# A two-part block (windowed attention, then token and channel mixing) on one core: the first attention tile in two halves of heads, conversions at other places in tiles 0, 7 and 8, and five clamps on GpSimd

## The chip, the cores and the metric

The kernel runs on one core of one Trainium2 chip. The metric is the device time of one execution in microseconds (us). The kernel before took 800.99 us, the median of three runs (800.95 to 801.45). The engines are called as in the profile: PE (matrix products), ACT (activations and copies), DVE (vector operations), POOL (GpSimd), SP (issues DMA transfers; ACT can issue them too).

## The reference

Eight sequences of 576 tokens with 8 heads of 64. First attention with a window of 64 tokens; then a mixing step over tokens (`w_tok1`, 576 to 256, and `w_tok2`, back), and one over channels (`w_ch1`, 512 to 1536, and `w_ch2`, back). All data are float32.

```python
scores = scale * np.matmul(q, k.transpose(0, 1, 3, 2))
mask = (rel >= 0) & (rel < window)                 # rel = query position - key position
scores = np.where(mask, scores, -1e9)
scores = scores - np.max(scores, axis=-1, keepdims=True)
attn = np.exp(scores)
attn = attn / (np.sum(attn, axis=-1, keepdims=True) + 1e-09)
x = np.matmul(attn, v)                             # heads side by side: (8, 576, 512)
h = np.maximum(xt @ w_tok1, 0.0) @ w_tok2          # xt is x with tokens and channels exchanged
u = x + h.transpose(0, 2, 1)
out = u + np.maximum(u @ w_ch1, 0.0) @ w_ch2
```

The four weights arrive as float64, as pairs of 32-bit words, and the kernel makes float32 numbers of them on the chip.

## The kernel before

**Attention in 36 tiles.** A tile is two blocks of 64 queries with all 8 heads; nine tiles hold a pair of sequences. One pass of the loop over `i` works on several tiles at once, and the order of the instructions on each engine is the order in which the loop writes them: every engine runs its own list in order and waits where its operand isn't there. For tile `i`:

- `qk` (L282) makes the scores on PE into two PSUM tiles `s` of four heads each: u=0 the even heads, u=1 the odd ones.
- `softmax` (L297) masks, negates and takes the row minimum of each head on DVE: one instruction for a head and a short one that reads out the minimum `nm`.
- `softmax_exp` (L305) makes the exponentials `e` on ACT, one instruction per head, with the row sums.
- `pt_transpose` transposes `e` on PE (L312, into `pp`) and copies it to SBUF on ACT (L314, `pt`).
- `av` multiplies by v on PE (L324, `xp`, in the PSUM slot "av"); `recip` (L333 on POOL in tiles 0 to 6, L336 on DVE) and `norm` (L341 on DVE) give the attention output `x`.
- `split_x` makes `xhi` on ACT (L109) and `xlo` on POOL (L112). `tok1` (L372, PE) adds the tile to the two PSUM banks `h` of its sequence with three products per bank. When a sequence is complete, `finish_h` (L383) takes the positive part of both banks to `hhi` on ACT, and `finish_h_low` (L392) the remainder `hlo` on DVE, which frees the banks. From tile 9 on `tok2` (L413, L420, PE; L425, ACT) makes the mixed tokens `u` from it, through one PSUM slot "up".

**Weight pieces.** Between the tiles the weights are converted in 28 pieces of 320 or 384 columns; `JOBS` says in which pass. Pieces 0 to 4 are converted in passes 0 to 4, pieces 5 and 6 in passes 7 and 8. A piece takes six DVE instructions: L204 (strip the sign), L206 (the clamp: a maximum and a minimum with constants), L207 (shift), L216, L218, L219; then POOL adds two parts to `w` (L221). In the next pass `job_finish` splits `w` into `t1hi` or `t2hi` on ACT (L109) and the remainder `t1lo` on POOL or `t2lo` on DVE (L112). On ACT this split stands ahead of that pass's exponentials. The first three DVE steps of a piece (L204, L206, L207) are `job_convert_a`, the last three (L216, L218, L219, with the sum `w` on POOL) `job_convert_b`; in passes below `N_START` = 7 both stand behind `norm`, in passes from 7 on both ahead of it.

**Stages behind it.** From about 250 us on come the channel products in two ways (three plain chunks, then pairs of chunks by a scheme with seven products in place of eight); the change doesn't touch them.

**The start.** SP loads q of tile 0, the k blocks of tile 0, q of tile 1, the k blocks of tile 1 and so on, while PE runs five products of zeros (L481).

Of the kernel before, what the change touches and what calls it, by code (L numbers as in the profile page):

```python
# [22 lines left out]
P = 128  # L23
# [24 lines left out]
N_START = 7  # L48
# [42 lines left out]
def mixer_kernel(ctx: ExitStack, tc: tile.TileContext, qh, kh, vh, wt1, wt2, wc1, wc2, out):  # L91
# [39 lines left out]
    with ExitStack() as actx:  # L131
# [64 lines left out]
        def to_f32_a(raw, n, tag, late=False):  # L196
# [9 lines left out]
            nc.vector.tensor_scalar(out=cf, in0=cf, scalar1=F64_LOW, scalar2=F64_HIGH, op0=ALU.max, op1=ALU.min)  # L206
            nc.vector.tensor_scalar(out=c, in0=c, scalar1=3, scalar2=0x3FFFFFFF,  # L207
                                    op0=ALU.logical_shift_left, op1=ALU.bitwise_and)
            return c, low, high, n, tag, late
# [31 lines left out]
        def job_convert_a():  # L241
            if to_convert:
                n, raw = to_convert.pop(0)
                to_convert_b.append((n, to_f32_a(raw, jobs[n][4], n, n >= N_FIRST)))
# [24 lines left out]
        def qk(i):  # L269

            qt = loaded[i][0]
            s = []
            for u in range(2):

                s.append(ps.tile([P, 4, P], F32, name=f"s{i}_{u}", tag="h" if i == 1 else "s", bufs=2))
                s_ps[i, u] = s[u]
            for j in range(4):
                for u in range(2):
                    r = slice(u * BLK, (u + 1) * BLK)
                    for half, (b, n) in enumerate(tile_blocks(i)):  # L280
                        so = s[u][half * BLK:(half + 1) * BLK, j].rearrange("p (n c) -> p n c", n=2)
# [3 lines left out]
        def softmax(i, u):  # L285
            if u == 0:
# [4 lines left out]
            e = pa.tile([P, 4, P], F32, name=f"e{i}_{u}", tag="e", bufs=4)  # L291
            e_sb[i, u] = e

            s = s_ps.pop((i, u))
            for h in range(4):
                g = 2 * h + u
                nc.vector.tensor_tensor_reduce(out=e[:, h], in0=s[:, h], in1=mk, scale=-scale, scalar=MAX_F32,  # L297
                                               op0=ALU.add, op1=ALU.min, accum_out=nm[:, g:g + 1])

        def softmax_exp(i, u):  # L300
            e = e_sb[i, u]
            nm, sm = st[i]
            for h in range(4):
                g = 2 * h + u
# [158 lines left out]
        load_q(0)  # L463
# [19 lines left out]
        for i in range(-1, NT + 1):  # L483
# [59 lines left out]
            for n in tok1_plan.get(i + 1, ()):  # L543
                if n not in xhl:
                    split_x(n)
# [548 lines left out]
```

## Time and profile before

| What | Value |
|---|---|
| median of three runs | 800.99 us |
| profiled execution | 801.79 us, of which the span of its instructions is 799.8 us |
| PE busy | 787.4 us, 98% of the span |
| DVE, ACT, POOL busy | 71%, 49%, 33% |
| granted PE clock | 1.00 in every window up to 800 us |
| PE busy in 5 to 45 us | 36.78 of 40.00 us |
| PE busy in 45 to 75 us | 27.24 of 30.00 us |
| PE busy in 75 to 250 us | 174.15 of 175.00 us |

A row of the timeline gives start and duration in us, engine, source line, operation, output<-inputs by the program's names, the shapes, and in brackets how long the engine had stood idle and what ended that. A row of the list of waits gives the sum of the idle time, how often, and the longest. An engine that waits behind another one's hold on the SBUF counts as busy.

### The profile page before, as it was taken

To read this page: it belongs to the slowest core of one execution; us is meant where nothing else is said; L and a number is where in the kernel's file an instruction comes from. 1 tells how busy PE (TensorE), PEld (TensorE's weight loads), DVE (VectorE), ACT (ScalarE), POOL (GpSimd) and SP (SyncE) were. 2 spreads that over 40 slices of the span, in tenths; PEclk is the share of its full clock that TensorE was granted. 3 is DMA by queue.
4 is the path that set the end of the run, shared out by engine and by line. 5 is a ranking of instruction groups with operands and counts; after the bars stand their busy time and mean duration, and the time that the engine had idled before them with its cause. 6 is when DMAs were issued, how large, how long until landed. Compare 5 with 4: busy or idle time off the path is not lost.

```text
span 799.8 us, 15811 instructions
## 1 busy us (share of the span) xinstructions
PE 787.4 (98%) x5749; PEld 654.8 (82%) x5749; DVE 570.2 (71%) x1533; ACT 388.3 (49%) x1124; POOL 262.5 (33%) x237
## 2 busy tenths in 40 slices
PE   8999999999999999999999999999999999999997
PEld 6667888888889888888888888888888888888886
DVE  5978789589582795777788474757766667656576
ACT  6999889889874441323334141326332244324040
POOL 3634545445330000000000050549732638723140
PEclk9999999999999999999999999999999999999999
DMA  9856779668635537877655775765985756955543
GB/s 352 282 179 229 235 251 304 223 217 308 218 113 170 197 103 216 257 225 235 207 164 193 275 289 184 258 236 203 294 320 201 288 187 207 349 209 191 201 159 105
DMA packets 86828, 180.59 MB, mean 226 GB/s; under 512 B 8800, under 2 KB 51808, under 8 KB 84832
## 3 DMA queue, kind: packets, MB, share of 16 engines
q1 hardware_dynamic: 84640, 177.76, 64.4%
q10 hardware_dynamic: 2112, 1.84, 0.7%
q8 instruction: 45, 0.74, 0.4%
q14 instruction: 31, 0.25, 0.1%
HBM read 137.69 MB, written 41.88 MB: 225 GB/s over the span
## 4 chain that ended last, share of the span: by engine, by line
PE 93%; ACT 3%; DVE 3%; POOL 1%; issue 1%; DVEq 0%; ACTq 0%
PE op L969 22%; PE gp L913 21%; PE op L643 12%; PE gp L635 12%; PE up L420 6%; PE h L372 6%; PE xp L324 4%; PE s L282 3%; PE pp L312 3%; PE up L413 3%; ACT e L305 2%; DVE e L297 1%; PE idle L481 1%; DVE x L341 1%; POOL xlo L112 0%
## 5 line engine op out<-in xcount | busy, mean ns | idle before, releaser
L913 PE MATMUL gp<-m,w1hi 128*128 128x512 f32 x504 | 155.1, 389 | 0.0
L112 POOL TENSOR_TENSOR m7lo<-t3g,m7hi 128x512 fp32r<-128x512 f32 x18 | 23.4, 1300 | 359.4 <-ACT m7hi L109 359.4
L305 ACT ACTIVATE e<-e,nm 128x128 f32<-128x128 f32 x288 | 112.3, 398 | 5.7 <-DVE nm L297 5.7
L913 PEld LDWEIGHTS gp<-m,w1hi 128*128 128x128 f32 x504 | 94.6, 188 | 19.6
L913 PE MATMUL gp<-m,w1lo 128*128 128x512 f32 x252 | 98.0, 389 | 0.0
L958 DVE TENSOR_TENSOR uf<-op,uf 128x512 f32<-128x512 f32 (+1 forms) x91 | 61.9, 684 | 39.5 <-PE op L969 31.7
L297 DVE CUSTOM_DVE_ANT_0 e<-s,mask 128x128 f32<-128x128 f32 x288 | 63.5, 286 | 12.5 <-PE s L282 12.4
L112 POOL TENSOR_TENSOR xlo<-x,xhi 128x512 fp32r<-128x512 f32 x32 | 41.2, 1289 | 46.3 <-ACT xhi L109 46.0
L305 ACT ACTIVATION_READ_ACCUMULATOR e<-e,nm 128x1 f32 x288 | 56.3, 196 | 0.0
L635 PE MATMUL gp<-ulo,w1hi 128*128 128x512 f32 x144 | 56.0, 389 | 0.0
L635 PE MATMUL gp<-uhi,w1hi 128*128 128x512 f32 x144 | 56.0, 389 | 0.0
L635 PE MATMUL gp<-uhi,w1lo 128*128 128x512 f32 x144 | 56.0, 389 | 0.0
L913 PEld LDWEIGHTS gp<-m,w1lo 128*128 128x128 f32 x252 | 47.3, 188 | 9.9
L916 ACT COPY x<-gp 128x512 f32<-128x512 f32 x18 | 10.6, 588 | 80.8 <-PE gp L913 80.8
L643 PE MATMUL op<-glo,w2hi 128*128 128x512 f32 x128 | 49.8, 389 | 0.0
L643 PE MATMUL op<-ghi,w2hi 128*128 128x512 f32 x128 | 49.8, 389 | 0.0
L643 PE MATMUL op<-ghi,w2lo 128*128 128x512 f32 x128 | 49.8, 389 | 0.0
L221 POOL TENSOR_TENSOR w<-r,c 128x384 f32<-128x384 f32 (+1 forms) x28 | 27.6, 985 | 59.8 <-DVE r L219 57.8
L324 PEld LDWEIGHTS xp<-v,pt 128*64 128x64 f32 x1152 | 36.6, 138 | 12.9 <-ACT e L305 10.1
L341 DVE TENSOR_TENSOR x<-xp,ri 128x512 f32<-128x512 f32 x36 | 24.9, 691 | 30.1 <-PE xp L324 29.5
L312 PE MATMUL pp<-ident,e 128*128 128x128 f32 x288 | 44.2, 281 | 1.3
L420 PE MATMUL up<-t2hi,hhi 128*128 128x320 f32 (+1 forms) x128 | 43.0, 336 | 0.0
(204 smaller groups left out, 2040.3 us busy)
## 6 DMA issues: line engine op xcount, KB each, us to landing
v<-vh SPq DMA_DIRECT2D x36, 512.0 KB, 4.0
w1hi<-w1s SPq DMA_DIRECT2D x18, 896.0 KB, 5.1
w1lo<-w1s SPq DMA_DIRECT2D x18, 896.0 KB, 7.1
w1hi<-w2s SPq DMA_DIRECT2D x18, 896.0 KB, 4.6
w1lo<-w2s SPq DMA_DIRECT2D x18, 896.0 KB, 6.4
raw<-wc SPq DMA_DIRECT2D x32, 384.0 KB, 4.3
q<-qh SPq DMA_DIRECT2D x36, 256.0 KB, 4.8
k<-kh SPq DMA_DIRECT2D x7, 1280.0 KB, 8.0
```

Source lines behind the costliest of these rows:

```text
L112: eng_lo.tensor_sub(lo, src, hi.bitcast(F32))
L297: nc.vector.tensor_tensor_reduce(out=e[:, h], in0=s[:, h], in1=mk, scale=-scale, scalar=MAX_F32, op0=ALU.add, op1=ALU.min, accum_out=nm[:, ...
L305: nc.scalar.activation(e[:, h], e[:, h], AF.Exp, bias=nm[:, g:g + 1], scale=-1.0, accum_out=sm[:, g:g + 1])
L312: nc.tensor.transpose(pp[:, h], e[:, h], ident)
L324: nc.tensor.matmul(xp[half * BLK:(half + 1) * BLK, h], pts[h % 2][:, h // 2, half * BLK:(half + 1) * BLK], vt[:, half, h], start=True, sto ...
L372: nc.tensor.matmul(h_ps[b][tt], w[:, o + tt * P:o + (tt + 1) * P], x, start=first and n == 0, stop=last and n == len(combos) - 1)
L420: nc.tensor.matmul(up[:, :n], hx[:, cs], w[:, tt * S + s0:tt * S + s0 + n], start=False, stop=(k == 6), skip_group_check=True)
L635: nc.tensor.matmul(gp, w[:, w1_at(ft, ct)], x[:, ct], start=(k == 0), stop=(k == 3 * NCT - 1))
L643: nc.tensor.matmul(op, w[:, ct, ft], x[:, cols], start=(first and k == 0), stop=(last and k == 3 * len(gs) - 1), skip_group_check=not (fir ...
L913: nc.tensor.matmul(b[INTO[m]], w[:, at], c[:, h, t], start=(k < 4 and z == y == 0), stop=(z == 1 and y == 2), skip_group_check=True)
L958: eng.tensor_add(x, y, x)
L969: nc.tensor.matmul(bank[:, cols], w[:, o:o + P], x[:, cols], start=(i == 0 and y == 0 and m in ("m1", "m6", "m7", "m5")), stop=(i == 1 and ...
```

## The change

- **First tile.** q and k of tile 0 are loaded in two parts, heads 0 to 3 and 4 to 7; of each part half of the k blocks comes through ACT's queue, and the k blocks of tile 1 do too. The scores of tile 0 go to four PSUM tiles (two more in the slots "h"), and its reductions and exponentials are done by halves of heads over both u. The scores of tile 1, which had the slots "h", go to "up" and "av".
- **Clamps on POOL.** `to_f32_a` is cut in two. The sign and the clamp (L204, L206) of pieces 1 to 4 are done at the end of the pass before, with the clamp on POOL; those of piece 0 in pass 0 ahead of `norm`, its clamp on POOL too.
- **Tiles 7 and 8.** `job_convert_b` moves from ahead of `norm` to behind `split_x` there (`N_SPLIT` = 9).
- **`finish_h`.** For sequences 0, 2, 4 and 6 the second `hhi` is taken on DVE, as a maximum with zero.

Lines of the changed kernel are shifted: L206 is the clamp on POOL, L210 the shift, L219, L221, L222 the former L216, L218, L219, L224 the sum `w`, L349 the former L333, L357 `norm`.

POOL's list, from its first work on tile 0 to the remainder of the second weight piece. Before (`ri` is the row sum plus a constant, `c` a piece under conversion, numbers tell buffers apart):

```order
L333 TENSOR_SCALAR ri_248<-sum_179 128x8
L221 TENSOR_TENSOR w_283<-r_282,c_278 128x320
L333 TENSOR_SCALAR ri_338<-sum_237 128x8
L112 TENSOR_TENSOR xlo_342<-x_276,xhi_341 128x512
L112 TENSOR_TENSOR t1lo<-w_283,t1hi 128x320
L221 TENSOR_TENSOR w_379<-r_378,c_374 128x320
L333 TENSOR_SCALAR ri_434<-sum_327 128x8
```

and now the same stretch:

```order
L349 TENSOR_SCALAR ri_254<-sum_185 128x8
L206 TENSOR_SCALAR c_265<-c_265 128x320
L224 TENSOR_TENSOR w_289<-r_288,c_265 128x320
L206 TENSOR_SCALAR c_294<-c_294 128x320
L349 TENSOR_SCALAR ri_349<-sum_243 128x8
L112 TENSOR_TENSOR xlo_353<-x_285,xhi_352 128x512
L112 TENSOR_TENSOR t1lo<-w_289,t1hi 128x320
L224 TENSOR_TENSOR w_387<-r_386,c_294 128x320
L206 TENSOR_SCALAR c_392<-c_392 128x320
```

A clamp of the next piece stands between each sum `w` and the `ri`, `xlo` and `t1lo` behind it.

DVE's list in pass 7, from the reciprocal to the reductions of the next tile. Before (`x_992` is the output of tile 7):

```order
L336 RECIPROCAL ri_936<-ri_936 128x8
L204 TENSOR_SCALAR c_943<-raw_608 128x384
L206 TENSOR_SCALAR c_943<-c_943 128x384
L207 TENSOR_SCALAR c_943<-c_943 128x384
L216 SCALAR_TENSOR_TENSOR c_943<-raw_608,c_943 128x384
L218 TENSOR_SCALAR r_969<-c_943 128x384
L219 SCALAR_TENSOR_TENSOR r_969<-raw_608,r_969 128x384
L341 TENSOR_TENSOR x_992<-xp_975,ri_936 128x512
```

and now:

```order
L352 RECIPROCAL ri_942<-ri_942 128x8
L204 TENSOR_SCALAR c_949<-raw_517 128x384
L206 TENSOR_SCALAR c_949<-c_949 128x384
L210 TENSOR_SCALAR c_949<-c_949 128x384
L357 TENSOR_TENSOR x_992<-xp_975,ri_942 128x512
L219 SCALAR_TENSOR_TENSOR c_949<-raw_517,c_949 128x384
L221 TENSOR_SCALAR r_1016<-c_949 128x384
L222 SCALAR_TENSOR_TENSOR r_1016<-raw_517,r_1016 128x384
```

The last three steps of the piece now stand behind `x` of the tile. POOL's list in passes 7 and 8, before:

```order
L221 TENSOR_TENSOR w_970<-r_969,c_943 128x384
L112 TENSOR_TENSOR xlo_1013<-x_992,xhi_1012 128x512
L221 TENSOR_TENSOR w_1072<-r_1071,c_1057 128x384
L112 TENSOR_TENSOR xlo_1115<-x_1094,xhi_1114 128x512
L112 TENSOR_TENSOR xlo_1217<-x_1192,xhi_1216 128x512
```

and now:

```order
L112 TENSOR_TENSOR xlo_1013<-x_992,xhi_1012 128x512
L224 TENSOR_TENSOR w_1017<-r_1016,c_949 128x384
L112 TENSOR_TENSOR xlo_1115<-x_1094,xhi_1114 128x512
L224 TENSOR_TENSOR w_1119<-r_1118,c_1063 128x384
L112 TENSOR_TENSOR xlo_1223<-x_1198,xhi_1222 128x512
```

Each sum `w` now stands behind the `xlo` of the same tile. ACT's list isn't moved: `t2hi` of the piece stands behind the two copies `pt` and ahead of the next exponentials, as before.

```diff
-        def to_f32_a(raw, n, tag, late=False):
+        def to_f32_abs(raw, n, tag, late, clamp):
...
-            nc.vector.tensor_scalar(out=cf, in0=cf, scalar1=F64_LOW, scalar2=F64_HIGH, op0=ALU.max, op1=ALU.min)
+            clamp.tensor_scalar(out=cf, in0=cf, scalar1=F64_LOW, scalar2=F64_HIGH, op0=ALU.max, op1=ALU.min)
+            return c, low, high, n, tag, late
+
+        def to_f32_a(c, *rest):
             nc.vector.tensor_scalar(out=c, in0=c, scalar1=3, scalar2=0x3FFFFFFF,
                                     op0=ALU.logical_shift_left, op1=ALU.bitwise_and)
-            return c, low, high, n, tag, late
+            return c, *rest
...
+            tags = (("up", 1), ("av", 1)) if i == 1 else (("s", 2), ("s", 2))
+            s = [ps.tile([P, 4, P], F32, name=f"s{i}_{u}", tag=tag, bufs=bufs) for u, (tag, bufs) in enumerate(tags)]
+            s_ps[i] = s + (s if i else [ps.tile([P, 4, P], F32, name=f"s{i}_{u + 2}", tag="h", bufs=2)
+                                        for u in range(2)])
...
+        def heads(i, part):
+            if i == 0:
+                return [(u, h) for u in range(2) for h in range(2 * part, 2 * part + 2)]
+            return [(part, h) for h in range(4)]
...
-                nc.scalar.activation(hi, h_ps[b][tt], AF.Relu)
+                if b % 2 == 0 and tt == 1:
+                    nc.vector.tensor_scalar(out=hi, in0=h_ps[b][tt], scalar1=0.0, scalar2=None, op0=ALU.max)
+                else:
+                    nc.scalar.activation(hi, h_ps[b][tt], AF.Relu)
...
-        nc.sync.dma_start(k0[:, :, :2], kh0[:, :, :2])
+        for part in range(2):
+            js = slice(part * 2, part * 2 + 2)
+            nc.sync.dma_start(q0[:, js], qh[0, :, js])
+            js = slice(part * 2 * BLK, (part + 1) * 2 * BLK)
+            for g, eng in enumerate((nc.sync, nc.scalar)):
+                eng.dma_start(k0[:, g, :2, js], kh0[:, g, :2, js])
         load_q(1)
-        nc.sync.dma_start(k0[:, :, 2:], kh0[:, :, 2:])
+        nc.scalar.dma_start(k0[:, :, 2:], kh0[:, :, 2:])
...
-            if i >= N_START:
+            if i >= N_SPLIT:
                 for _ in range(n_jobs):
                     job_convert_b()
+            if i == 0:
+                job_convert_abs(nc.gpsimd)
             if 0 <= i < NT:
                 norm(i, av(i, pts), ri)
...
                     job_convert_a()
                     job_convert_b()
+                if n_jobs and JOBS[i + 1]:
+                    job_convert_abs(nc.gpsimd)
             if i + 2 < NT:
                 qk(i + 2)
             for n in tok1_plan.get(i + 1, ()):
                 if n not in xhl:
                     split_x(n)
+            if N_START <= i < N_SPLIT:
+                for _ in range(n_jobs):
+                    job_convert_b()
             run_pieces(min(have, n_pieces[1]))
```

More of the change, by code (lines that the diff above doesn't have):

```diff
@@ L46 @@
 TOK1_FROM, TOK1_SLOW, TOK2_FROM = 2, 7, 9
-N_START = 7
+N_START, N_SPLIT = 7, 9
 NX = 4
@@ L290, in softmax, with softmax_exp @@
             mk = mask[1 if tile_blocks(i)[0][1] == 0 else 0]
[L291 to L295, printed above, removed]
+            for u, h in heads(i, part):
+                if (i, u) not in e_sb:
+                    e_sb[i, u] = pa.tile([P, 4, P], F32, name=f"e{i}_{u}", tag="e", bufs=4)
                 g = 2 * h + u
[L297 to L301, printed above, removed]
+                nc.vector.tensor_tensor_reduce(out=e_sb[i, u][:, h], in0=s_ps[i][h // 2 * 2 + u][:, h], in1=mk,
+                                               scale=-scale, scalar=MAX_F32, op0=ALU.add, op1=ALU.min,
+                                               accum_out=nm[:, g:g + 1])
+        def softmax_exp(i, part):
             nm, sm = st[i]
-            for h in range(4):
-                g = 2 * h + u
+            for u, h in heads(i, part):
+                e, g = e_sb[i, u], 2 * h + u
                 nc.scalar.activation(e[:, h], e[:, h], AF.Exp, bias=nm[:, g:g + 1], scale=-1.0,
```

28 lines of the change are left out of this document (16 added, 12 removed).

## The prediction

> **What bounds the kernel now.** First the page's head, to see which engine is full, and the sums of the chain of waits, to see who sets the end:
>
> ```profile
> PE 787.4 (98%) x5749; PEld 654.8 (82%) x5749; DVE 570.2 (71%) x1533; ACT 388.3 (49%) x1124; POOL 262.5 (33%) x237
> PE 93%; ACT 3%; DVE 3%; POOL 1%; issue 1%; DVEq 0%; ACTq 0%
> ```
>
> PE is busy 98% and holds 93% of the chain. Nothing in the change shortens PE's own work, so only PE's idle time can be won or made longer. The windows tell where it lies:
>
> ```profile
> 5.00:45.00 40.00, 36.78 (x558) 26.08 (x559) 33.59 (x172) 35.25 (x141) 19.48 (x27) 1.00 0.89 321
> 45.00:75.00 30.00, 27.24 (x405) 21.98 (x401) 24.16 (x119) 26.06 (x101) 10.39 (x9) 1.00 0.60 210
> 75.00:250.00 175.00, 174.15 (x2370) 153.30 (x2369) 133.32 (x576) 148.78 (x548) 74.73 (x64) 1.00 0.68 229
> ```
>
> After the stretch's length stand the busy times of PE, its weight loads, DVE, ACT and POOL, then the granted clock (1.00, so no clock effect). PE lacks 3.2 us in the first stretch, 2.8 in the second, 0.9 in the third. From 75 us on it is practically continuous, so what the first ten tiles gain or lose moves the end one for one. In the first stretch ACT (35.25 of 40) and DVE (33.59) are nearly full too: PE's busy time is stretched there, and the loop runs at the pace of the ring between DVE, POOL and ACT worked out in part B.
>
> **The change, part by part.** *A, the first tile.* Here and below stand those rows of an engine's timeline that are used (start, duration, engine, line, operation, in brackets the idle time before it and what ended that):
>
> ```profile
> 5.73 1.47 PE L282 MATMUL s<-k,q 64*64 64x128 f32 x32
> 8.51 1.10 PE L282 MATMUL s<-k,q 64*64 64x128 f32 x32 [1.30 <-DMA k<-kh]
> 11.41 1.22 PE L324 MATMUL xp<-v,pt 128*64 128x64 f32 x32
> 11.44 0.20 DVE L336 RECIPROCAL ri<-ri 128x8 f32<-128x8 f32 x1
> 12.68 0.69 DVE L341 TENSOR_TENSOR x<-xp,ri 128x512 f32<-128x512 f32 x1 [1.05 <-PE xp L324]
> 13.29 0.32 DVE L204 TENSOR_SCALAR c<-raw 128x320 int32<-128x320 int32 x1
> 13.64 0.33 DVE L206 TENSOR_SCALAR c<-c 128x320 f32<-128x320 f32 x1
> 16.73 0.46 ACT L109 CAST t1hi<-w 128x320 fp32r<-128x320 f32 x1 [0.23 <-POOL w L221]
> ```
>
> The scores of tile 0 take 1.47; with half the heads ready the reductions can start about 0.74 earlier. That doesn't reach `x` of tile 0. Tile 1's scores still wait for their k (8.51), and they now fill the slots "up" and "av", so `xp` of tile 0, in "av", cannot start before DVE has reduced tile 1. Those reductions end where the reciprocal starts, 11.44, and `xp` started at 11.41: `x` stays at 12.68. What is won stands behind `x`: L204 and L206 of piece 0 (13.29 to 14.00 with their gaps, 0.71) move ahead of it, where DVE idles 1.05 us for `xp`. With that cover gone they would cost 0.71 again, and the part nothing. So L207 starts 0.7 earlier, and with it `w` and `t1hi` (16.73): **-0.70**. The bounds are -1.2 and 0: how the k parts land through ACT's queue in shorter runs no row shows; a delay would have to pass the 1.30 wait to matter, and I allow half a microsecond either way, and the slot's wait the other 0.2.
>
> *B, the rings of tiles 1 to 4.* A pass lasts from one `w` (21.34) to the next (26.87), 5.53 us:
>
> ```profile
> 21.34 0.88 POOL L221 TENSOR_TENSOR w<-r,c 128x320 f32<-128x320 f32 x1 [2.04 <-DVE r L219]
> 22.62 1.27 POOL L112 TENSOR_TENSOR xlo<-x,xhi 128x512 fp32r<-128x512 f32 x1
> 23.85 0.98 POOL L112 TENSOR_TENSOR t1lo<-w,t1hi 128x320 fp32r<-128x320 f32 x1
> 26.87 0.88 POOL L221 TENSOR_TENSOR w<-r,c 128x320 f32<-128x320 f32 x1 [2.04 <-DVE r L219]
> ```
>
> ```profile
> 23.80 0.32 DVE L204 TENSOR_SCALAR c<-raw 128x320 int32<-128x320 int32 x1
> 24.15 0.87 DVE L206 TENSOR_SCALAR c<-c 128x320 f32<-128x320 f32 x1
> 25.05 0.33 DVE L207 TENSOR_SCALAR c<-c 128x320 int32<-128x320 int32 x1
> 25.41 0.49 DVE L216 SCALAR_TENSOR_TENSOR c<-raw,c 128x320 int32<-128x320 int32 x1
> 25.94 0.33 DVE L218 TENSOR_SCALAR r<-c 128x320 int32<-128x320 int32 x1
> 26.30 0.49 DVE L219 SCALAR_TENSOR_TENSOR r<-raw,r 128x320 f32<-128x320 uint32 x1
> ```
>
> L206 takes 0.33 alone (13.64) and 0.87 here: it overlaps `t1lo` on POOL (23.85 to 24.83) and ends 0.19 behind it. I read this as DVE held off the SBUF until `t1lo` is nearly done. The ring is then `w` to `xlo` 1.28 (with the short `ri` between), to `t1lo` 1.23, to the end of L206 1.17, and L207 to the next `w` 1.85: 5.53. Now L206 is gone from DVE and stands on POOL as the clamp, of length c, between `w` and `ri` and so ahead of `xlo`. L207 fits between `xlo` and `t1lo`; L216 takes L206's place as the one held by `t1lo`, ends likewise 0.19 behind it, and L218, L219 and the gaps follow (0.33, 0.49 and 0.11). The new ring is 1.28 + c + 1.23 + 1.17 + 0.04 + 0.33 + 0.03 + 0.49 + 0.07, and some 0.17 for the hold's end that falls in L216's longer body: 4.81 + c.
>
> No row has a one-input operation with two constants on POOL. The nearest:
>
> ```profile
> L221 POOL TENSOR_TENSOR w<-r,c 128x320 f32<-128x320 f32 x4 | 3.5, 876 | 10.7 <-DVE r L219 10.7
> L265 POOL CAST t1z<-t1lo 64x256 fp32r<-64x256 f32 x2 | 0.8, 418 | 0.1
> L177 POOL COPY swapped<-ident 128x64 f32<-128x64 f32 x2 | 0.4, 238 | 0.1
> ```
>
> A line through the two one-input rows (0.238 at 64 columns, 0.418 at 256) gives 0.48 at 320; the lower bound is 0.42, the upper the two-input 0.88. The clamp reads one operand, so I take 0.48. The ring becomes 5.29, 0.24 less, four times: -0.96. Of it I give back 0.4, since the two `t1z` casts (0.84 together) lie beside DVE's steps in pass 4 and hold them once the ring is shorter (bounds 0 and 0.84): **-0.55**. At c = 0.42 and nothing given back it is -1.2; at 0.88 it is 4 x 0.16 + 0.4 = +1.0; the sign turns at c = 0.62. The Trainium skill, "GPSIMD Engine Reference", section "4.1 Engine selection", speaks against the edit: an elementwise max on a tile belongs on VectorE. Its section "3.1 Elementwise — side-by-side cycle accounting" gives 1.8 cycles per element at best and 2.6 with two inputs, at 1.2 GHz; with the 0.24 of the small copy that would be, as an estimate, c = 0.71 or 0.93, and B about +0.4 or +1.2. No run here shows which.
>
> *C, hhi on DVE for even sequences.*
>
> ```profile
> 49.02 0.47 PE L372 MATMUL h<-xlo,t1hi 128*128 128x512 f32 x1 [0.97 <-DVE hlo L392]
> 101.71 0.44 PE L413 MATMUL up<-ident,x 128*128 128x128 f32 x2 [0.45 <-ACT u L425]
> 162.76 0.44 PE L413 MATMUL up<-ident,x 128*128 128x128 f32 x2 [0.28 <-ACT u L425]
> ```
>
> The first sequence gains nothing: PE waits at 49.02 for `hlo` of the first bank, which stands behind the first `hhi`, still on ACT. Later ACT has one `hhi` less ahead of its copies `u`, and the two waits on them, 0.73, can go. Bounds 0 and -0.73; **-0.6**. DVE's extra instruction lies in a stretch where DVE is busy 76%.
>
> *D, tiles 7 and 8,* by the rows of DVE, POOL, ACT and PE:
>
> ```profile
> 54.14 0.69 DVE L341 TENSOR_TENSOR x<-xp,ri 128x512 f32<-128x512 f32 x1
> ```
>
> ```profile
> 54.14 1.00 POOL L221 TENSOR_TENSOR w<-r,c 128x384 f32<-128x384 f32 x1 [3.63 <-DVE r L219]
> 55.56 1.28 POOL L112 TENSOR_TENSOR xlo<-x,xhi 128x512 fp32r<-128x512 f32 x1 [0.42 <-ACT xhi L109]
> 61.80 1.28 POOL L112 TENSOR_TENSOR xlo<-x,xhi 128x512 fp32r<-128x512 f32 x1 [0.25 <-ACT xhi L109]
> ```
>
> ```profile
> 54.87 0.62 ACT L109 CAST xhi<-x 128x512 fp32r<-128x512 f32 x1 [1.68 <-DVE x L341]
> 56.71 0.53 ACT L109 CAST t2hi<-w 128x384 fp32r<-128x384 f32 x1
> 57.13 0.41 ACT L305 ACTIVATE e<-e,nm 128x128 f32<-128x128 f32 x1
> ...
> 63.00 0.41 ACT L305 ACTIVATE e<-e,nm 128x128 f32<-128x128 f32 x1
> 67.78 0.37 ACT L425 COPY u<-up 128x256 f32<-128x256 f32 x1
> ```
>
> ```profile
> 68.46 0.38 PE L413 MATMUL up<-ident,x 128*128 128x128 f32 x2
> ```
>
> Before, `w` of piece 5 was done (55.14) ahead of `xhi`'s end, and `t2hi` followed the copies `pt`. Times now from the start of `x` of tile 7 (54.14 before). I grant that `x` no gain from the three steps that leave its front: it follows `xp` on PE. `xlo` stays at 1.42 to 2.70, since it waits for `xhi`. L219 overlaps it and ends, held, at 3.1. `w` runs 3.15 to 4.15, `t2hi` 4.2 to 4.6. Behind `t2hi` on ACT stand all exponentials of tile 9: they start at 4.6, 2.99 before, 1.6 late. They take 3.1 (eight of the row's 0.41, each begun a little before the one ahead ends), so `xhi` of tile 8 runs 7.7 to 8.3 and its `xlo` 8.35 to 9.65 (ended at 63.08 before, 8.94, so PE gets it 0.7 late). The second piece adds: `w` 10.05 to 11.05, `t2hi` to 11.5, so the exponentials of tile 10 start at 11.5, 8.86 before (63.00), 2.6 late. The copy `u` (67.78) stands behind them on ACT, 2.5 late, and with it the second "up" on PE (68.46, 14.32 before, 16.5 now): **+2.2**. The lower bound is 1.3, if L219 isn't held by `xlo` and `w` starts at 2.7; the upper 2.6. Nothing gives it back: PE is full from there.
>
> **The sum.** -0.70 - 0.55 - 0.6 + 2.2 = +0.35. The profiled execution took 801.79, with 2.0 of it around the span; it becomes 802.1. The median of the runs is 0.80 lower, so 800.99 + 0.35 = **801.3 us**.
>
> **Rivals.** *One, faster: D is absorbed.* PE lacked 2.76 us between 45 and 75 us; if the later exponentials fall into waits that PE has anyway, the sum is -1.85: 799.1. For it: `x` of tile 7 may come earlier with three steps out of its way. Against: ACT's order holds the exponentials behind `t2hi` whatever PE does. Chance 0.18.
>
> *Two, slower: the clamp runs at the two-input pace.* The place is POOL, between `w` and `ri` of tiles 1 to 4; it decides from c = 0.62 on. At 0.88, B is +1.0 and the sum +1.9: 802.9. For it: every 128-partition operation of that width on POOL took 0.88 or more. Against: the `t1z` casts are faster per column. Chance 0.14.
>
> *Three: transfers.* The k of tile 1 lands later, since other transfers now come between; its 1.30 wait grows by 0.5 to 1, which eats A: about 802.1. Chance 0.08.
>
> **How the numbers follow.** The forecast holds 0.57, and 0.03 stays for sums of several. The median is told from no change at about 0.2%, 1.6 us: 799.4 to 802.6. The forecast's own range, from the bounds of its terms, is 800.2 to 802.5, nearly all "same". Faster: most of rival one and a little of the forecast, 0.19. Slower: most of rival two, a third of three, and the forecast's tail, 0.22. Same: the rest, 0.59. From 799.0 to 803.1 the range takes in the middle of one and two and leaves out what goes beyond.
>
> **What would show it.** A: L207 of piece 0 right behind `x`, `x` still near 12.7; `t1hi` at 16.0. B: the clamp's mean on POOL near 0.48, `w` to `w` 5.3, L216 stretched in place of L206. C: no wait of PE for `u` near 101 and 162. D: on ACT `t2hi` 4.2 behind `x` of tile 7, ended by a wait for POOL's `w`, and PE's idle time between 45 and 75 us up by about 2 us. The forecast is wrong if `w` overtakes there, if c is over 0.62, or if `x` of tile 0 itself moves.

## The result and the profile after

The changed kernel took 805.98 us, the median of six runs (804.47 to 806.69), against 801.07 for the kernel before beside it: a ratio of 1.0058, interval 1.0045 to 1.0071. It is 4.9 us slower, where no change was forecast, and outside the range of 799.0 to 803.1. The page's head and the sums of the chain of waits, of the changed kernel:

```profile
PE 790.2 (98%) x5749; PEld 657.9 (82%) x5749; DVE 572.5 (71%) x1532; ACT 386.7 (48%) x1120; POOL 268.4 (33%) x242
PE 92%; DVE 3%; POOL 1%; ACT 1%; DMA 1%; issue 1%; SPq 0%; DVEq 0%; ACTq 0%
```

Its windows, as for the kernel before:

```profile
5.00:45.00 40.00, 34.09 (x519) 25.68 (x520) 29.88 (x149) 31.30 (x124) 23.81 (x29) 0.91 0.83 299
45.00:75.00 30.00, 26.93 (x346) 20.03 (x341) 23.22 (x111) 24.50 (x96) 9.84 (x10) 0.94 0.61 206
75.00:250.00 175.00, 174.92 (x2425) 154.06 (x2424) 138.22 (x605) 149.31 (x558) 76.99 (x67) 1.00 0.69 230
```

PE is busy 2.7 us less in the first 45 us, and POOL 4.3 us more. The granted clock, 1.00 in these three stretches before, is 0.91 and 0.94 in the first two. The list of waits of PE has one new large row, the second half of tile 0's k:

```profile
PE s L294 <- DMA k<-kh: 3.4, 1, 3.4
```

One row of the kernel before is gone:

```profile
PE up L413 <- ACT u L425: 0.7, 2, 0.4
```

What follows is told by a ledger. It takes six moments of the profiled execution of each kernel: the starts of `x` of tiles 0, 7, 10 and 35 on DVE, of `w` of pieces 0 and 4 on POOL, and the end of the span. Between `x` of tile 0 and `w` of piece 0 lies the early clamp; from there to `w` of piece 4 lie the four rings; from `x` of tile 7 to that of tile 10 the conversions of part D; from there to tile 35 part C. The executions of one kernel spread by up to 4.5 us in some of these runs, and the profiled one of the changed kernel (806.69) was the slowest of its six, so the ledger goes with the median, not in its place.

| Kernel (us) | x 0 | w 0 | w 4 | x 7 | x 10 | x 35 | span |
|---|---|---|---|---|---|---|---|
| before | 12.68 | 15.83 | 38.42 | 54.14 | 72.08 | 241.63 | 799.8 |
| changed | 15.36 | 17.78 | 42.54 | 58.24 | 78.50 | 246.70 | 804.7 |
| difference | +2.68 | +1.95 | +4.12 | +4.10 | +6.42 | +5.07 | +4.9 |

So the first tile lost 1.95 us (a gain of 0.70 was forecast), the four rings 2.17 (forecast: a gain of 0.55), tiles 7 to 10 2.32 (forecast 2.2), and from tile 10 on 1.35 came back (forecast 0.6).

**The first tile.** Rows of PE and, last two, of DVE:

```profile
5.01 0.67 PE L294 MATMUL s<-k,q 64*64 64x128 f32 x16
9.12 2.84 PE L294 MATMUL s<-k,q 64*64 64x128 f32 x48 [3.44 <-DMA k<-kh]
```

```profile
15.36 0.69 DVE L357 TENSOR_TENSOR x<-xp,ri 128x512 f32<-128x512 f32 x1 [1.19 <-PE xp L340]
15.97 0.32 DVE L210 TENSOR_SCALAR c<-c 128x320 int32<-128x320 int32 x1
```

The first half of the scores starts 0.7 us earlier than tile 0 did before, but the second half waits 3.4 us for its k. The clock in short windows (the number behind the five busy times):

```profile
8.00:9.00 1.00, 0.00 (x0) 0.00 (x0) 0.00 (x0) 0.00 (x0) 0.00 (x0) 0.50 1.03 414
9.00:14.00 5.00, 4.76 (x58) 4.09 (x59) 2.84 (x26) 2.35 (x10) 0.23 (x1) 0.50 1.04 398
69.00:72.00 3.00, 3.00 (x43) 2.27 (x45) 1.08 (x4) 2.98 (x12) 0.00 (x0) 0.51 0.48 197
```

While PE idles the clock falls to half, and it stays there for some five microseconds of work: 48 products take 2.84 us, where 64 took 2.57 before (1.47 and 1.10). It falls a second time from 69 to 72 us.

How much this costs differs between executions. Three more traced kernels below load tiles 0 and 1 in the same way (clamps on DVE, other operations on POOL, tiles 7 and 8 without the split): their waits for the second half are 2.2, 2.4 and 3.0 us, their `x` of tile 0 comes at 14.30, 14.53 and 15.23, and the clock is at half for 3.4, 3.4 and 6.8 us (6.8 in the changed kernel's trace, from 7.6 to 14.5). So the 15.36 of the ledger is the late end of this spread.

**The rings.** POOL, then DVE, in one ring:

```profile
23.79 0.88 POOL L224 TENSOR_TENSOR w<-r,c 128x320 f32<-128x320 f32 x1 [1.32 <-DVE r L222]
24.64 1.28 POOL L206 TENSOR_SCALAR c<-c 128x320 f32<-128x320 f32 x1
26.00 0.24 POOL L349 TENSOR_SCALAR ri<-sum 128x8 f32<-128x8 f32 x1
26.32 1.27 POOL L112 TENSOR_TENSOR xlo<-x,xhi 128x512 fp32r<-128x512 f32 x1
27.55 0.94 POOL L112 TENSOR_TENSOR t1lo<-w,t1hi 128x320 fp32r<-128x320 f32 x1
29.82 0.88 POOL L224 TENSOR_TENSOR w<-r,c 128x320 f32<-128x320 f32 x1 [1.32 <-DVE r L222]
```

```profile
27.19 0.59 DVE L210 TENSOR_SCALAR c<-c 128x320 int32<-128x320 int32 x1
27.82 1.03 DVE L219 SCALAR_TENSOR_TENSOR c<-raw,c 128x320 int32<-128x320 int32 x1
```

The clamp takes 1.28 us, not 0.48. The ring is 6.03; the prediction's 4.81 + c gives 6.09. L219 (L216 of before) is stretched to 1.03 by `t1lo`, and ends 0.36 behind it.

**Tiles 7 to 10.** POOL, ACT, PE:

```profile
59.66 1.27 POOL L112 TENSOR_TENSOR xlo<-x,xhi 128x512 fp32r<-128x512 f32 x1 [5.53 <-ACT xhi L109]
61.43 1.02 POOL L224 TENSOR_TENSOR w<-r,c 128x384 f32<-128x384 f32 x1 [0.49 <-DVE r L222]
```

```profile
62.47 0.51 ACT L109 CAST t2hi<-w 128x384 fp32r<-128x384 f32 x1 [1.55 <-POOL w L224]
62.89 0.40 ACT L321 ACTIVATE e<-e,nm 128x128 f32<-128x128 f32 x1
...
69.02 0.51 ACT L109 CAST t2hi<-w 128x384 fp32r<-128x384 f32 x1 [1.47 <-POOL w L224]
69.43 0.40 ACT L321 ACTIVATE e<-e,nm 128x128 f32<-128x128 f32 x1
```

```profile
74.89 0.38 PE L432 MATMUL up<-ident,x 128*128 128x128 f32 x2
```

From the start of `x` of tile 7 (58.24): `w` at 3.19, `t2hi` at 4.23, the exponentials of tile 9 at 4.65 and of tile 10 at 11.19, the second "up" at 16.65. Forecast were 3.15, 4.2, 4.6, 11.5 and 16.5.

### The profile page after: what moved, and what is told of

It reads as the page before. It is cut to its first block, busy times and chain, and to the rows that moved or that the text cites. A ratio compares the mean times of both kernels' runs of the same rounds, so it can differ in the third digit from the quotient of the medians.

```text
span 804.7 us, 15813 instructions
## 1 busy us (share of the span) xinstructions
PE 790.2 (98%) x5749; PEld 657.9 (82%) x5749; DVE 572.5 (71%) x1532; ACT 386.7 (48%) x1120; POOL 268.4 (33%) x242
## 4 chain that ended last, share of the span: by engine, by line
PE 92%; DVE 3%; POOL 1%; ACT 1%; DMA 1%; issue 1%; SPq 0%; DVEq 0%; ACTq 0%
PE op L1001 21%; PE gp L945 21%; PE op L675 12%; PE gp L667 12%; PE up L439 6%; PE h L388 6%; PE xp L340 4%; PE s L294 4%; PE pp L328 3%; PE up L432 3%; ACT e L321 1%; DMA k<-kh 1%; DVE x L357 1%; DVE c L219 1%; POOL w L224 1%
## 5 line engine op out<-in xcount | busy, mean ns | idle before, releaser
L294 PE MATMUL s<-k,q 64*64 64x128 f32 x1152 | 43.3, 284 | 5.0 <-DMA k<-kh 3.4
L224 POOL TENSOR_TENSOR w<-r,c 128x384 f32<-128x384 f32 (+1 forms) x28 | 27.6, 986 | 48.1 <-DVE r L222 46.1
```

Source lines behind the costliest of these rows:

```text
L294: nc.tensor.matmul(so, qt[r, j, half], kbs[b][r, n:n + 2, j], start=True, stop=True)
```

## The experiments

All medians are beside runs of the kernel before on the same chip (801.4 to 801.7); the ratio is to those.

**Is it the transfers?** Loads of tiles 0 and 1 as before, the rest as changed:

```diff
+        load_q(0)
...
-        for part in range(2):
-            js = slice(part * 2, part * 2 + 2)
-            nc.sync.dma_start(q0[:, js], qh[0, :, js])
-            js = slice(part * 2 * BLK, (part + 1) * 2 * BLK)
-            for g, eng in enumerate((nc.sync, nc.scalar)):
-                eng.dma_start(k0[:, g, :2, js], kh0[:, g, :2, js])
+        nc.sync.dma_start(k0[:, :, :2], kh0[:, :, :2])
         load_q(1)
-        nc.scalar.dma_start(k0[:, :, 2:], kh0[:, :, 2:])
+        nc.sync.dma_start(k0[:, :, 2:], kh0[:, :, 2:])
```

> The changed kernel, with q and k of tiles 0 and 1 loaded as before: whole, through SP only; the halves of heads stay. Theory 'shared transfers' (the second half of k waits behind the k of tile 1, which goes through ACT's queue at the same time): PE's wait of 3.4 us and the half clock from 9 to 14 us are gone, x of tile 0 is back near 12.7 (15.36 now), its first w near 15.1 (17.78): 2.6 us less, median 803.3. Rival 'the halves and the slot av themselves cost': x of tile 0 stays later than 13.5 and less than 1.5 us are given back, median over 804.5.

Measured: 805.28, ratio 1.0043 (1.0031 to 1.0055), with single runs from 803.69 to 806.54. In the profiled execution (803.91) `x` of tile 0 is at 12.53 and `w` of piece 0 at 14.95: 2.83 less than in the changed kernel. The moments came as the theory said, and the rival's mechanism, `x` later than 13.5, falls. The median didn't come down as far: it is 3.7 above the kernel before, where the changed kernel is 4.9 above, which is the rival's number and not the theory's 803.3. In the runs above 805 the mean clock of the execution was 0.996 against 0.999 in the profiled one, which speaks for longer half clock there; these runs have no trace, so the place and the cause aren't shown. The halves of heads, with whole loads, bring nothing that can be told: `x` of tile 0 lies at 12.53 and 12.27 in the two kernels with halves and whole loads, and between 11.80 and 12.68 in those with tile 0 whole and the same loads.

Then only the k of tile 1 back on SP, the parts kept:

```diff
-        nc.scalar.dma_start(k0[:, :, 2:], kh0[:, :, 2:])
+        nc.sync.dma_start(k0[:, :, 2:], kh0[:, :, 2:])
```

> The changed kernel, with only the k of tile 1 back in SP's queue behind q of tile 1. Theory 'shared transfers' (2048-byte packets of that k on ACT's queue, 84 ns each, alternate with the 512-byte packets of the second half on SP's queue, 27 ns each): PE's wait for the second half falls from 3.4 us to under 1.2, x of tile 0 comes at 13.5 or before (15.36), median 804 to 805. Rival 'the parts themselves are slow' (512-byte packets, twice as many): the wait stays at 2.5 us or more, median 805.5 to 806.

Measured: 806.36, ratio 1.0056 (1.0043 to 1.0069), as slow as the changed kernel. The theory holds for the half and fails for the sum (it looked for 804 to 805):

```profile
5.74 1.49 PE L294 MATMUL s<-k,q 64*64 64x128 f32 x32
9.62 1.74 PE L294 MATMUL s<-k,q 64*64 64x128 f32 x32 [2.39 <-DMA k<-kh]
```

Tile 0's scores now run through without a wait, so the second half had been late because of the k of tile 1 beside it. But now that k is late: 9.62, against 8.51 before. It is issued at 3.13, behind five DMAs of about 0.45 each on SP, where it stood behind three, at 2.13, before; one microsecond later issued, one later there. `x` of tile 0 gains 0.7 (14.66), and the clock is still at 0.66 from 9 to 12 us. Whichever queue it is in, what tile 0 waits for in the end is the last of the two tiles' k.

**Is it the clock?** Eight products of zeros between the two halves:

```diff
             for j in range(4):
+                if i == 0 and j == 2:
+                    for _ in range(8):
+                        nc.tensor.matmul(idle, zero[:, :P], zero, start=True, stop=True)
```

> The changed kernel, with eight products of zeros on PE between the two halves of tile 0's scores (some 3 us of work where PE waited 3.4 us). Theory 'the clock falls because PE idles': the granted clock is 1.00 from 9 to 15 us (0.50 to 0.59 now), the 48 products from 9.1 us on take 1.7 us and not 2.84, x of tile 0 comes about 1.3 earlier, 804.7. Rival 'the clock falls whatever PE does' or 'PE isn't the limit there': x at 15 or later, 806.

Measured: 807.4, ratio 1.0072 (1.006 to 1.0084). The products took more than the wait:

```profile
6.80 3.83 PE L292 MATMUL idle<-zero 128*128 128x256 f32 x16
10.56 1.54 PE L297 MATMUL s<-k,q 64*64 64x128 f32 x48
```

```profile
9.00:12.00 3.00, 3.00 (x56) 2.39 (x54) 0.74 (x7) 0.41 (x4) 0.00 (x0) 1.00 1.05 406
```

The clock stays at 1.00, the 48 products take 1.54 in place of 2.84, and although they start 1.44 us later, `x` of tile 0 comes at 15.31 as before (15.36). So the idling is what lowered the clock at the first tile, and the half clock cost about 1.5 (1.44 + 0.05) of the 2.7 us that tile 0 lost in these two traces. As a remedy it gave nothing here, since the filling was too long. Up to tile 35 (246.72) the kernel is level with the changed one; the end is 1.7 later, of which a late wait of PE for ACT shows 0.7; the rest wasn't followed up. The fall at 69 us is no whole idle stretch: PE waited 0.18 and 0.92 us in the three microseconds ahead of it, and the eight transposes before them took 2.01 us in place of 1.09, so PE waited inside that group too. The Trainium skill, "TensorE: Matmul & The Clock Gate", section "Part 1: The HAM clock gate (the "warmup" mystery)", says that the clock goes to half after an idle window of about 3.4 us and comes back after as long a busy one. By the rows less was enough both times: the clock was at half by 8.0 us, 2.3 after PE's last product had ended (5.68), and at 69 us PE had never stood still for a whole microsecond. The way back, some five and 3.4 us of work, is nearer to the page.

What decides isn't shown. Of the seven traced kernels with the split, two (the loads as before, the clamps on DVE) had the same two waits (0.18 and 0.93 or 0.94) and the same long transposes (2.02 and 1.99) and stayed at 1.00. And in a kernel told below, the kernel before with `hhi` and the early L204 and L206, PE waited 2.18 us at the first tile without a fall and 2.24 us, up to 24.4 us, with one.

**What does POOL ask for a clamp?** The five clamps on DVE at their new places (the edit is made at both calls):

```diff
-                job_convert_abs(nc.gpsimd)
+                job_convert_abs(nc.vector)
```

> The changed kernel, with the five clamps back on DVE at their new places. Theory 'price of the clamp' (the clamp took 1.28 us on POOL and lengthened each ring from 5.53 to 6.02): the rings fall to 5.1 to 5.3 us, since POOL's part is then 0.97 + 0.31 + 1.23 + 1.17 + L216's tail and DVE takes 0.36 more; four rings give back 3 us or more, median 802.4 to 803. Rival 'only the late start counts': the rings come back to no less than 5.53, 2 us are given back and the median is 804 or more. If the clamp isn't the cause at all: 806.

Measured: 805.72, ratio 1.0043 (1.0026 to 1.0059), single runs 802.07 to 806.55. The rings are 5.39 and 5.40, near the theory's 5.1 to 5.3, and the four together 22.10, 2.66 less than in the changed kernel; so the clamp on POOL is the cause of the longer rings. `w` of piece 4 is at 38.82, 3.7 earlier, but 1.06 of this is the earlier start of `x` of tile 0 (14.30), which the edit doesn't touch. The gain holds to tile 35 (242.68, 4.0 earlier). Yet the profiled span ends at 803.3, only 1.4 earlier, and the median is far from the theory's 802.4 to 803. What took the rest in the trace is told below, under the held sum.

Other operations on POOL in place of three clamps (this kernel leaves the clamp of pieces 1 to 3 out in whole or in part):

```diff
+            if tag == 1:
+                clamp.tensor_scalar(out=cf, in0=cf, scalar1=F64_LOW, scalar2=None, op0=ALU.max)
+            elif tag == 2:
+                clamp.tensor_copy(cf, cf)
+            elif tag == 3:
+                clamp.tensor_scalar(out=cf, in0=cf, scalar1=1.0, scalar2=None, op0=ALU.mult)
+            else:
+                clamp.tensor_scalar(out=cf, in0=cf, scalar1=F64_LOW, scalar2=F64_HIGH, op0=ALU.max, op1=ALU.min)
```

> The changed kernel, with other operations in place of three of the five clamps on POOL, on the same 128x320 columns: piece 1 a maximum with one constant, piece 2 a copy, piece 3 a multiplication by 1.0; pieces 0 and 4 keep the maximum and minimum. It leaves the clamp out in part. Theory 'each constant costs': the clamp of 1.28 us is 0.19 + 3.4 ns a column, two operations of 1.7 ns; the maximum alone takes 0.7 to 0.8, the multiplication the same, the copy 0.48 (the line of the prediction). Rival 'every arithmetic one-input operation takes 1.28': maximum and multiplication 1.28, copy 0.48. Each ring is shorter than 6.02 by what its operation is shorter.

Measured, in one run (804.88), rows of POOL:

```profile
16.95 0.88 POOL L231 TENSOR_TENSOR w<-r,c 128x320 f32<-128x320 f32 x1 [2.04 <-DVE r L229]
17.81 1.00 POOL L207 TENSOR_SCALAR c<-c 128x320 f32<-128x320 f32 x1
...
22.70 0.89 POOL L231 TENSOR_TENSOR w<-r,c 128x320 f32<-128x320 f32 x1 [1.32 <-DVE r L229]
23.54 0.44 POOL L209 COPY c<-c 128x320 f32<-128x320 f32 x1
...
27.89 0.89 POOL L231 TENSOR_TENSOR w<-r,c 128x320 f32<-128x320 f32 x1 [1.31 <-DVE r L229]
28.86 1.01 POOL L211 TENSOR_SCALAR c<-c 128x320 f32<-128x320 f32 x1
```

A copy takes 0.44, a maximum or a multiplication with one constant 1.00, both constants of the clamp 1.28. Neither theory had that: the first operation costs 0.56 over a copy, the second 0.28. The line through a copy and a cast that gave 0.48 was near for a copy and told nothing of arithmetic. The rings follow the formula 4.81 + c: 5.75 with the maximum (5.81 by the formula), 5.19 with the copy (5.25), 5.88 with the multiplication (5.82). The Trainium skill, "GPSIMD Engine Reference", section "4.1 Engine selection", has one-input operations at roughly line rate on GpSimd. Here the copy (0.44) comes nearest to that, beside 0.33 for the clamp on DVE; the arithmetic doesn't, since it was slower than the two-input sum `w` (0.88).

**Tiles 7 and 8.** The changed kernel without the split:

```diff
-N_START, N_SPLIT = 7, 9
+N_START, N_SPLIT = 7, 7
```

> The changed kernel, with the last three steps of the pieces in tiles 7 and 8 ahead of norm again (N_SPLIT = 7). Theory 'w behind xlo' : the exponentials of tile 9 start 3.0 us behind the start of x of tile 7 (4.65 now), the second product into 'up' 14.3 behind it (16.65 now): 2.3 us less, no half clock near 70 us, median 803.7. Rival 'PE would have waited anyway': under 0.8 us less, median over 805.2.

Measured: 803.04, ratio 1.0018 (1.0009 to 1.0026); from `x` of tile 7 to that of tile 10 17.95 us (20.26 in the changed kernel, 17.94 before), without a half clock there. The first theory holds. And the split alone, on the kernel before:

```diff
-            if i >= N_START:
+            if i >= N_SPLIT:
                 for _ in range(n_jobs):
                     job_convert_b()
...
+            if N_START <= i < N_SPLIT:
+                for _ in range(n_jobs):
+                    job_convert_b()
```

> The kernel before, with the last three steps of the pieces in tiles 7 and 8 behind norm and xlo (N_SPLIT = 9) and nothing else changed. Theory 'w behind xlo': x of tile 10 comes 2.1 later against x of tile 7 than before, and all of it is still there at the last tile; median 803.5. Rival 'it costs only on top of the other delays': under 0.8, median under 802.2.

Measured: 803.85, ratio 1.0028 (1.0017 to 1.0039), 2.2 us; `x` of tile 7 to tile 10 20.14, 2.20 more than before, and from there to tile 35 no change. The rival falls. The clock is at half for 3.4 us near 63 us in this trace; in the two with the split where it isn't, the same stretch takes 20.07 and 20.06, so by this comparison the half clock is 0.1 to 0.2 of the 2.2 to 2.3.

**hhi alone,** on the kernel before:

```diff
-                nc.scalar.activation(hi, h_ps[b][tt], AF.Relu)
+                if b % 2 == 0 and tt == 1:
+                    nc.vector.tensor_scalar(out=hi, in0=h_ps[b][tt], scalar1=0.0, scalar2=None, op0=ALU.max)
+                else:
+                    nc.scalar.activation(hi, h_ps[b][tt], AF.Relu)
```

> The kernel before, with the second hhi of sequences 0, 2, 4 and 6 on DVE and nothing else changed. Theory 'all of the late gain is this part' (between 69 and 250 us the changed kernel won back 1.4 of its 6.4 us): 1.4 us less than before, median 799.7. Rival 'only the two listed waits for u go': 0.7 less, 800.4. Rival 'the late gain was slack that a later start fills': no change, 801.1.

Measured: 800.88, ratio 0.9991 (0.9982 to 0.9999). From `x` of tile 10 to that of tile 35 it wins 1.31, as the changed kernel did (1.35), in three steps of 0.35 to 0.5 near 101, 162 and 221 us. So the first theory holds up to tile 35; of the gain 0.7 is left in the median, which is the size of its rival, and what took the rest isn't shown. The step near 221 had no row in the list of waits. Its cost stood inside a row: the eight transposes there, of the kernel before and of this one:

```profile
221.39 1.43 PE L312 MATMUL pp<-ident,e 128*128 128x128 f32 x8
```

```profile
219.97 1.09 PE L312 MATMUL pp<-ident,e 128*128 128x128 f32 x8
```

0.34 us more for the same eight products: PE waited ahead of the last of them, and the group counts as busy.

**All together, and the held sum.** The changed kernel with loads, clamps and tiles 7 and 8 undone (the diffs above):

> The changed kernel with three parts undone: loads of tiles 0 and 1 whole and through SP, the five clamps on DVE (at their new places), N_SPLIT = 7. Left are the halves of heads and hhi. Theory 'three causes that add up' (late k, clamp on POOL, w behind xlo): with rings of 5.40 (5.53 before), the first w 0.4 to 0.9 earlier and 1 us from hhi, 799.2. Rival 'the halves and the slot av cost something of their own': 801.5 or more.

And the kernel before with hhi and the earlier L204 and L206, both on DVE, but tile 0 whole:

```diff
+            if i == 0:
+                job_convert_abs()
             if 0 <= i < NT:
                 norm(i, av(i, pts), ri)
...
+                if n_jobs and JOBS[i + 1]:
+                    job_convert_abs()
```

> The kernel before with two things of the change: hhi on DVE for even sequences, and L204 and L206 of pieces 0 to 4 earlier, both on DVE. Tile 0 whole, its loads and slots as before, conversions of tiles 7 and 8 as before. Theory: the first w 0.7 earlier, rings 5.40, hhi 1 us: 798.9, and the same as with the halves within 0.5. Rival 'halves of heads help': 0.5 or more above the run with the halves.

Measured: 801.81 (ratio 1.0001, 0.9992 to 1.0009) and 801.78 (0.9999, 0.9989 to 1.0009). Both theories looked for 799. So the three parts together are what made the changed kernel slower; but the gain that was to be left over isn't there. In the first, tile 35 did come 2.66 us earlier than before (238.97), and the end not at all (799.8). DVE's row of that place in the run with the clamps on DVE, and POOL beside it:

```profile
669.82 7.01 DVE L990 TENSOR_TENSOR uf<-u,uf 128x512 f32<-128x512 f32 x1
```

```profile
668.74 2.56 POOL L826 TENSOR_TENSOR m<-t,m 128x512 fp32r<-128x512 f32 x2
671.25 2.54 POOL L990 TENSOR_TENSOR uf<-u,uf 128x512 f32<-128x512 f32 x2
673.74 2.54 POOL L826 TENSOR_TENSOR m<-r,m 128x512 fp32r<-128x512 f32 x2
```

A sum of two SBUF operands that takes 0.69 elsewhere lasts 7.01 us, until POOL's unbroken row of operations ends at 676.3; in the run with three parts undone it is 7.00, from 666.08. The sums that free PSUM banks stand behind it on DVE, and PE waits 1.4 us for one. In the kernel before the same sum got through, about where the first of two operations on POOL ended, and POOL's pair took longer:

```profile
667.53 3.08 POOL L794 TENSOR_TENSOR m<-t,m 128x512 fp32r<-128x512 f32 x2
668.76 0.69 DVE L958 TENSOR_TENSOR uf<-u,uf 128x512 f32<-128x512 f32 x1
```

In the changed one it went in the same way (673.83, POOL's pair 3.09). POOL had idled 0.19 and 0.20 us shortly before in these two, and not in the held ones. But it isn't needed: in the second kernel of this part POOL hadn't idled either, and the sum got through in 0.74. What goes with the outcome is the moment of the request. Counted from the start of POOL's pair it came at 1.08 and 1.12 in the two held sums, at 1.13 in the one of 0.74, and at 1.22 to 1.24 in the nine traces where it took 0.69. No run set this moment by itself, so it isn't shown to be the cause. In these traces, then, a front that runs at other times met a late stage that took the gain back: with the clamps on DVE tile 35 is 1.05 later than before and the end 3.5. The Trainium skill, "SBUF — State Buffer", section "SBUF: two separate sides", says that a DVE operation with two SBUF inputs and one of GpSimd exclude each other for a whole instruction, and that who starts first has it; the rows agree that the two exclude each other, and show that POOL can win many times in a row.

In the second kernel the early L204 of piece 2 met its own data late:

```profile
21.30 1.30 DVE L204 TENSOR_SCALAR c<-raw 128x320 int32<-128x320 int32 x1 [1.51 <-DMA raw<-wt]
```

DVE waited 1.51 us, with the reductions of the next tile behind it, PE waited 2.24 us, its clock went to half from 25.0 to 28.4 us, and two rings took 7.94 and 6.06 us. Tile 35 is thus level with the kernel before (241.66).

The medians of these two hide single executions near 799 (798.95 in one of 11; 798.93, 799.53 and 799.69 in three of 12); they have no trace.

Both delays were taken away: the late data by leaving L204 and L206 of piece 2 where they were, the held sum first by giving it to POOL:

```diff
+                if n_jobs and JOBS[i + 1] and i != 1:
...
-                        add(c22, u2)
+                        add(c22, u2, eng2)
```

> The kernel before with hhi on DVE for even sequences; L204 and L206 earlier, on DVE, for pieces 0, 1, 3 and 4 (not for piece 2, whose raw data came 1.5 us after L204 asked for it in an earlier run); and in the last stage the sum of an output with u2 on POOL in place of DVE (there DVE was held for 7.0 us behind an unbroken row of operations on POOL in two earlier runs). Theory 'late raw and the held sum ate the gain': x of tile 35 comes 2.7 us earlier than before and this is still there at the end; median 798.7. Rival 'the late stage takes back what comes early': 801 or more.

Measured: 800.54, ratio 0.9988 (0.9979 to 0.9997). Tile 35 is 2.66 earlier, the end 1.4: half of what the theory asked for. POOL, with more to do, lets PE wait elsewhere (0.5 us for `m`); the other 0.8 isn't accounted for. With the k of tile 1 whole through ACT's queue on top:

```diff
-        nc.sync.dma_start(k0[:, :, 2:], kh0[:, :, 2:])
+        nc.scalar.dma_start(k0[:, :, 2:], kh0[:, :, 2:])
```

> The same, with the k of tile 1, whole, through ACT's queue. Theory 'the place in the queue sets when k lands' (each DMA that SP issues ahead of it delays it by 0.45): PE's wait for k of tile 1 (1.3 to 1.7) falls under 0.7, x of tile 0 comes 0.5 to 1 earlier, median 798.0. Rival 'the transfers share one rate': tile 0's own k lands later by as much, x of tile 0 as before or later, median 798.7 or more.

Measured: 801.48, ratio 0.9998 (0.9989 to 1.0007). The rival holds: PE no longer waits for tile 1, but starts tile 0 at 6.63 (5.65 without this), and `x` of tile 0 comes 1.0 later. Then the held sum stayed on DVE, but was issued behind a sum that frees a bank, with its control on the kernel before:

```diff
                     if final:
-                        add(c22, u2)
                         add(c12, u2, eng2)
                         add(c21, u2, eng2)
-                        store(3, c22)
                 elif m == "m2":
                     add(c11, bank)
                     store(0, c11)
+                    if final:
+                        add(c22, u2)
+                        store(3, c22)
```

> The kernel before with hhi on DVE for even sequences, L204 and L206 of pieces 0, 1, 3 and 4 earlier on DVE, and in the last stage the sum of an output with u2 on DVE as before, but issued behind the sum that frees a PSUM bank for PE. Theory 'what the front gains is lost only through the held sum': the last tile comes 2.7 us earlier, a held sum no longer stands ahead of the sums that PE waits for, and the end comes 2.3 us or more earlier: median 799.0. Rival 'the late stage takes it back in other places': the end comes at most 1.5 us earlier, 800 or more.

> The kernel before with only the sum with u2 issued later in the last stage. Both theories: no change, 801.5, since no sum was held there in the profile of the kernel before; if moving the sum itself costs or gains over 0.5, that has to be taken off the other run.

Measured: 799.23, ratio 0.997 (0.9959 to 0.998), and 801.98, ratio 1.0004 (0.9995 to 1.0013). Tile 35 comes 2.28 earlier than in the kernel before and the span ends 2.3 earlier; the control shows that moving the sum brings nothing by itself. In this trace the sum takes 1.4 us at most. So with the held sum out of the way the whole gain of the front reaches the end, and this version is faster than both kernels, by 0.3% over the one before: hhi on DVE, the early sign and clamp on DVE (but for piece 2), and one sum moved; without halves, without the clamp on POOL, without the split.

## Why the prediction was wrong

- **What bounds the kernel** held: PE's waits in the first 75 us set the time, and in the changed kernel the delays there moved the end one for one (5.07 at tile 35, 4.9 at the end). It isn't a rule: with three parts undone the last stage took back a gain of 2.66, and with the clamps on DVE it added 2.5 to a delay of 1.05.
- **A, the first tile,** is the first failed step. The early L204 and L206 did what was said: from `x` to `w` of piece 0 2.42 in place of 3.15, 0.73 less (forecast 0.70). That `x` stays at 12.68 was wrong by 2.68. The rest of the step, "a delay would have to pass the 1.30 wait to matter, and I allow half a microsecond either way", was a size without a row. The delay was 3.4 us at PE, from tile 1's k in the second queue, and about half of its cost was the clock, which the prediction had set aside as "no clock effect" because no window of the kernel before showed less than 1.00. Rival three named the transfers, but priced them at 0.5 to 1 us and for the k of tile 1, not for the second half.
- **B, the rings,** is the second. The formula for the ring was right to 0.08 us with four values of c. c was not: 1.28 against 0.48, and even the upper bound, 0.88, lay below it. The bounds came from a copy, a cast and a two-input sum, and none of these holds arithmetic with constants. With c = 1.28 the working gives +0.56 a ring; measured are +0.50 in three rings and +0.66 in the last. Rival two, the slower clamp, was thus the right mechanism, at a price too low. The 0.4 given back for the `t1z` casts can't be seen apart: the working priced four equal clamps, but the clamp of the last ring has 384 columns and took 1.50, 0.22 more, which alone is more than the 0.16 by which that ring lost more than the others. The estimate that the prediction gives as 0.71 comes to 0.72 by its own terms; nothing hangs on it.
- **C** was right in its place and half in its size: -1.35 at tile 35, not -0.6. The prediction added up the listed waits; the wait near 221 us was hidden in a row counted as busy (0.34), and the step near 162 was 0.49 where the list had 0.28.
- **D** was right to 0.15 us: 2.32, or 2.20 alone, against 2.2, with each step of the chain within about 0.3 us of where it was put. Of the 2.32, 0.1 to 0.2 is half clock, which wasn't in the working; in the two traces with the split and no fall the stretch takes 2.1 more than before, which is as near. One of its signs failed: PE's idle time from 45 to 75 us, said to rise by about 2, rose by 0.3 (3.07 against 2.76), because waits inside the transposes and the slower products count as busy. Rival one, that PE absorbs it, falls.
- The forecast's sum of +0.35 becomes, with the measured terms, +1.95 + 2.17 - 1.35 + 2.32 = +5.09.
- **The range.** The worst bounds of the four terms add up to 0 + 1.0 + 0 + 2.6 = +3.6, or 804.6; the stated upper end, 803.1, lay below even that. The measured time lies beyond both, since A and B each passed their bound (+1.95 against 0, +2.17 against +1.0): rivals two and three came true together, each at a higher price than it had been given.

## What to carry to other kernels

Price an operation on an engine from the same kind of operation there: on GpSimd a copy was no measure of arithmetic (0.44 against 1.00 and 1.28 here), and a bound from unlike rows is no bound. A load that is split or moved to a second queue is priced with everything that is then in flight beside it and behind it in the queue, and with the clock that PE may lose while it idles. Where a chain through several engines is written out from rows, as in B and D, it holds to a few tenths; what comes out earlier at the front is only won when the later stages are looked at too, above all where DVE and GpSimd work side by side.

## What the runs showed of the hardware

- GpSimd took 0.44 us for a copy of 128x320, 0.88 for a sum of two operands, 1.00 for one operation with a constant and 1.28 for two (1.50 at 128x384).
- A DVE sum of two SBUF operands was held for 7.0 us behind GpSimd operations without a gap, where in other executions it got through between two of them in 0.69 (0.74 in one without a gap either).
- While PE waited 3.4 us, its granted clock fell to half and stayed there for about five microseconds of work. Near 69 us, with no single wait above 0.92, it fell once more, for 3.4 us; in two other traces with the same waits it didn't. Where products of zeros filled the first wait, the clock stayed at 1.00.
- Each DMA at the head of SP's queue took about 0.45 us of it; two more ahead of a load brought it one microsecond later.
